# Masked attention with a feed-forward layer in float32 parts: the low part of k meets only the high part of q, as two 64-row matmuls, and eight feed-forward chunks are kept instead of eleven

## The chip, the cores and the metric

The kernel runs on one core of a Trainium2 chip. The metric is the device time of one execution in microseconds (us). The engines of the core are TensorE (PE, with its weight loads shown apart as PEld), VectorE (DVE), ScalarE (ACT), GpSimd (POOL) and SyncE (SP, which here only issues DMAs).

## The reference

Eight batches of eight heads, 576 positions, 64 numbers per head. A score survives only if it lies within tau = 0.02 of the greatest of its row; the rest of the row is masked. The result of attention, laid side by side by head, goes through a feed-forward layer with a leaky activation. All is float32 (the weights arrive as float64).

```python
scores = scale * np.matmul(q, k.transpose(0, 1, 3, 2))        # (8, 8, 576, 576), scale 1/8
thresh = np.max(scores, axis=-1, keepdims=True) - tau
scores = np.where(scores >= thresh, scores, -1000000000.0)
attn = np.exp(scores - np.max(scores, axis=-1, keepdims=True))
attn = attn / (np.sum(attn, axis=-1, keepdims=True) + 1e-09)
x = np.matmul(attn, v)                                        # heads side by side: (4608, 512)
h = x @ w_in                                                  # (512, 2048)
out = (np.maximum(h, 0.0) + alpha * np.minimum(h, 0.0)) @ w_out   # (4608, 512)
```

## The kernel before

**Parts.** A fast float32r matmul keeps only part of a float32's digits, so an operand is split into a high part (its rounded copy) and a low part (what is left), and products of parts are added in PSUM. For the scores of one head the stationary operand `qst` holds q's high part in rows 0 to 63 and q's low part in rows 64 to 127. The moving operands `kh` and `kl` hold the high and the low part of k, each twice, one above the other. So one 128-row matmul with `kh` gives (q high + q low) times k high, and one with `kl` gives (q high + q low) times k low.

**Pairs, units, cycles.** Two heads of one batch form a pair; there are 32 pairs. The 576 queries of each head are four chunks of 128 and a rest of 64; the two rests form one joint "tail" unit, so that a pair has nine units (`UNITS`). The attention loop runs over 288 cycles, one per unit, with a few before and behind. In cycle i it queues the masking of unit i, the scores of unit i+2, the row maximum and exponential of a unit ahead, the transposes of unit i (`turn`, `turn_k`, four or five 128-wide transposes by TensorE) and the copies of their results into parts (`hi`, `lo`). The scores of one unit are 576 keys as two halves of 288 columns in two PSUM banks: two matmuls with `kh`, two with `kl` (line 395); the tail has twice as many. `ps_s` holds the scores of two units.

**Beside the softmax.** In four of a pair's nine cycles the products with v are queued (`avmul`, line 542, the cycles `AVS`). The first four pairs (`WHOLE`) run them unsplit in float32 with a 128x64 stationary operand, all others in float32r parts with a 128x128 one. q, k and v of a later pair are loaded, split and moved into place at set cycles (`PREP`): `prep_qh`, `prep_qs` and `prep_ql` make q's parts (the low part in the tile `qt`), `move_q` and `move_q2` carry them by DMA from one half of the partitions to the other. The first pair is prepared by `prep_first`.

**The order of the work** on PE, ACT, DVE and POOL is written out by hand in the attention loop: each engine does its work in the order in which the loop queues it. SP's DMAs are in program order too.

**The planner of the feed-forward layer.** The 2048 hidden features are 16 chunks of 128. The first seven (`F1`) are worked off partly beside attention, for groups of 256 tokens, as soon as the batches they come from are done: layer 1 of one chunk is twelve 256-column matmuls (line 194, `pha`), layer 2 is 42 512-column matmuls per group, three parts by seven chunks by two halves (line 224, `acca`). `Mlp.cycle` decides in each cycle how much to queue. It holds a budget: `room` grows by `CYCLE` = 2.6 less the planned TensorE time of the cycle, `used`; a layer-1 chunk costs 1.31 of it, a layer-2 matmul 0.216. Its rule for layer 1, which also shows where the number of kept chunks enters:

```python
self.room = min(self.room, TH3) + CYCLE - used
if self.l1 and i >= self.gap and self.live < GB:
    ...
    elif slot and self.room > TH1 and ("i", fcs1[self.l1[0][2]]) in ready:
```

`live` counts chunks whose layer 1 is queued and whose second half of layer 2 is not; `GB` is both its limit and the number of buffers of the tile `g` (2 KB per partition each) that holds a chunk between the layers. `slot` is false in the four cycles with `avmul`.

**Behind attention.** `drain` does what the planner left of the first seven chunks, while the other nine chunks' weights are fetched and decoded from float64 (`Split64`, on ACT, DVE and POOL). Then the nine chunks are run for nine groups of 512 tokens (`phb`, `accb`). There the order is the compiler's scheduler's.

Of the kernel before, what the change touches and what calls it, by code (L numbers as in the profile page):

```python
# [11 lines left out]
F32R = mybir.dt.float32r  # L12
# [3 lines left out]
AF = mybir.ActivationFunctionType  # L16
ALU = mybir.AluOpType
AX = mybir.AxisListType
PSUM = bass.MemoryType.PSUM
DRAM = bass.MemoryType.DRAM  # L20

P = 128
D = 64
S = 576
NKC = 4
F1 = 7
G1 = 256
G2 = 512
# A float64's upper word read as a float32 orders values by magnitude. These two
# bounds are the words of the least normal float32 and of the largest one that  # L30
# still rounds to a finite 12-bit part.
WORD_LO = 2.0**-15
WORD_HI = 122876.0
ENGINES = {mybir.EngineType.PE, mybir.EngineType.Activation, mybir.EngineType.DVE, mybir.EngineType.Pool}
UNITS = [(0, 0), (0, 1), (1, 0), (1, 1), ("t", 0), (2, 0), (2, 1), (3, 0), (3, 1)]
GB = 11
ENG1 = ('vpp', 'vpp')
# [27 lines left out]
def f(ap):  # L65
    return ap.bitcast(F32)
# [3 lines left out]
def tile_masked_attention_moe(  # L70
# [11 lines left out]
    nc = tc.nc  # L82
# [19 lines left out]
    class Split64:  # L102
        """float64 bits -> hi + lo in float32r, to 24 bits or better."""

# [129 lines left out]
    at = ExitStack()  # L234
# [4 lines left out]
    KW = 2 * S + D  # L239
    qst_b = [ap1.tile([P, 2, S + D], F32R, name=f"qst{i}") for i in range(2)]  # L240
    for t in qst_b:
        nc.gpsimd.memset(f(t[:, :, S:]), 0.0)

    class Turned:
        """The transposed scores of two heads, in parts, with columns of ones that sum v."""

# [20 lines left out]
    class Pair:  # L267
        """The steps of two heads of one batch; each queues work on one or two engines."""

# [7 lines left out]
        def load(self, what):  # L277
            pi, b, hp = self.pi, self.b, self.hp
            if what == "v" and self.whole:
                self.vst = ap1.tile([P, 10, D], F32, tag="vst", name=f"vst{pi}", bufs=2)  # L280
                nc.sync.dma_start(self.vst, v[b, hp])
                return
            if what == "v":
                self.vr = ap1.tile([P, 10, D], F32, tag="raw", name=f"vr{pi}", bufs=2)
                nc.sync.dma_start(self.vr, v[b, hp])
                return
            src = (k if what == "k" else q)[b, hp]
            w = S + D if what == "k" else S
            if pi == 0:
                # The first pair's are doubled on the way in, so that its scores start at once.  # L290
                r = ap1.tile([P, KW if what == "k" else 2 * S], F32, tag="vst" if what == "k" else "p", name=f"{what}r{pi}", bufs=2)
                for j in range(2):
                    n = w if j else S
                    for half in range(2):
                        nc.sync.dma_start(r[half * D : (half + 1) * D, j * S : j * S + n], src[j * D : (j + 1) * D, :n])
                if what == "k":
                    self.kr = r
                else:
                    self.qr = r[:, : 2 * S].rearrange("p (a b) -> p a b", a=2)
                return  # L300
            if pi == 1:
                r = spool.tile([P, w], F32, name=f"{what}r{pi}")
            else:
                r = ap1.tile([P, w], F32, tag="raw", name=f"{what}r{pi}", bufs=2)
            nc.sync.dma_start(r, src[:, :w])
            if what == "k":
                self.kr = r
            else:
                self.qr = r

        def prep_first(self, j):
            """The splits of q and k for one head, before there is other work."""
            if j == 0:
                self.kh = ap1.tile([P, KW], F32R, tag="kh", name=f"kh{self.pi}", bufs=2)
                self.kl = ap1.tile([P, KW], F32R, tag="kl", name=f"kl{self.pi}", bufs=2)
                self.qst = qst_b[self.pi % 2]
            c = slice(0, S) if j == 0 else slice(S, KW)
            nc.scalar.activation(self.kh[:, c], self.kr[:, c], AF.Copy)
            nc.vector.tensor_tensor(self.kl[:, c], self.kr[:, c], f(self.kh[:, c]), op=ALU.subtract)
            qs = self.qst[:, j, :S]  # L320
            nc.scalar.activation(qs, self.qr[:, j], AF.Copy, scale=0.125)
            nc.vector.scalar_tensor_tensor(qs[D:], self.qr[D:, j], 0.125, f(qs[D:]), op0=ALU.mult, op1=ALU.subtract)

        # The two heads' q and k come one above the other. The parts are made so, and then moved:
        # qst holds the parts of q one above the other, kh and kl each part of k twice.
        def prep_kh(self):
# [16 lines left out]
        def prep_qh(self):  # L343
            self.qst = qst_b[self.pi % 2]
            nc.scalar.activation(self.qst[:, 0, :S], self.qr, AF.Copy, scale=0.125)

# [5 lines left out]
        def prep_ql(self):  # L352
            self.qt = ap1.tile([P, S], F32R, tag="qt", name=f"qt{self.pi}", bufs=1)
            if QLV and self.pi >= QLV:
                nc.vector.scalar_tensor_tensor(self.qt, self.qr, 0.125, f(self.qst[:, 0, :S]), op0=ALU.mult, op1=ALU.subtract)
                return
            nc.gpsimd.tensor_tensor(self.qt, self.qr, f(self.qst[:, 0, :S]), op=ALU.subtract)

        def move_q(self):
            nc.sync.dma_start(f(self.qst[:D, 1, :S]), f(self.qst[D:, 0, :S]))  # L360
            nc.sync.dma_start(f(self.qst[D:, 1, :S]), f(self.qt[D:]))

        def move_q2(self):
            nc.sync.dma_start(f(self.qst[D:, 0, :S]), f(self.qt[:D]))

# [10 lines left out]

        # A unit is (chunk of queries, head), or the tail: the last queries of the
        # first head above the first queries of the second.
        def scores(self, u):
            qc, j = UNITS[u]  # L380
            if u == 0:
                self.sm = ap1.tile([P, 9], F32, tag="sm", name=f"sm{self.pi}", bufs=2)
            qf = self.qst.rearrange("p a b -> p (a b)")
            key = lambda j, rot: (j * S + rot, j * S + rot + S)
            if qc == "t":
                stats = [(qf[:, NKC * P : S + D], key(0, 0)), (qf[:, S : S + P], key(1, D))]
            else:
                o = j * (S + 2 * D) + qc * P
                stats = [(qf[:, o : o + P], key(j, 0))]
            ps = ps_s.tile([P, 2, 512], F32, tag="s", name=f"s{self.pi}_{u}")  # L390
            n = len(stats)
            for ki, kk in enumerate((self.kh, self.kl)):
                for i, (w, (a, _)) in enumerate(stats):
                    for h in range(2):
                        nc.tensor.matmul(  # L395
                            ps[:, h, :288],
                            w,
                            kk[:, a + h * 288 : a + (h + 1) * 288],
                            start=(ki == 0 and i == 0),
                            stop=(ki == 1 and i == n - 1),  # L400
                        )
            self.S[u] = ps
# [39 lines left out]
        def turn_k(self, u):  # L442
            """The keys beyond the four blocks: of both heads at once for a chunk of queries."""
            qc, j = UNITS[u]
# [12 lines left out]
        def places(self, u):  # L457
            """(PSUM, its place in SBUF by part) for the unit's transposed blocks."""
            qc, j = UNITS[u]
# [96 lines left out]

        # Divide by the sums; rows that kept no score get the mean of v.
        def recip(self):
# [47 lines left out]

    # Where in a pair's nine cycles the work beside the softmax falls.
    for p in pairs:
        o = 9 * p.pi
        n = o - 9  # L610
# [36 lines left out]
    class Mlp:  # L647
        """The part of the MLP that runs beside attention, a little in each cycle."""

# [63 lines left out]
        def cycle(self, i, used, slot):  # L713
            """Work for the tensor engine up to the cycle's length."""
            self.room = min(self.room, TH3) + CYCLE - used
# [12 lines left out]
        def drain(self):  # L728
            """What is left when attention is done, in the scheduler's order."""
            for gi, st, fi in list(self.l1):  # L730
# [38 lines left out]
    nready = 0  # L769
    # The words of a piece of w_in wait where w_out's parts will be; those of w_out  # L770
    # in the place of its next chunk.
    pieces = []
# [18 lines left out]
    with tc.manual_schedule(engines=ENGINES) if ENGINES else ExitStack():  # L791
# [12 lines left out]
        for i in range(-3, total + TAIL):  # L804
# [17 lines left out]
            while nready < len(groups1) and sum(groups1[nready]) <= (i - RDY) // (9 * NPAIR) * S:  # L822
                mlp.ready(nready)
                nready += 1
            used = 0.92
            if unit(i + 2)[1] == 4:
                used += 0.49
            if unit(i)[1] in (1, 3, 4, 6, 8):
# [128 lines left out]
```

## Time and profile before

| | us |
|---|---|
| median of 3 runs | 1398.17 |
| lowest, highest | 1396.24, 1400.92 |
| span of the profiled execution | 1397.3 |
| DVE busy | 975.7 |
| ACT busy | 820.9 |
| POOL busy | 762.3 |

The profile is of one execution; its span, first instruction to last, is 0.9 us below the median of the runs, and no other time of that execution is given. Times of the trace are counted from the span's start. A matmul's duration in the trace is that from its start to a modelled end and holds the way through the array; matmuls overlap, so the time that one takes of TensorE is the distance between the starts (or the ends) of neighbours. A figure in brackets is the time an engine was idle before a row and what it waited for; "issue" means that the profile shows nothing it waited for.

### The profile page before, as it was taken

The numbers are of one execution on the slowest core, as the hardware profiler recorded it, in microseconds if no ns is written. First come the engines' busy times: TensorE is split into PE (matmuls) and PEld (weight loads), VectorE is DVE, ScalarE is ACT, GpSimd is POOL, SyncE is SP. The second block draws the span as 40 slices with busy tenths as digits, with TensorE's granted clock in tenths as the row PEclk, the third lists the DMA queues.
The fourth block names the chain that finished last, engine by engine and source line by source line (L and its number), as shares of the span: only waits on it lengthen the run. The fifth ranks groups of instructions, "written<-read, shape, count | busy, mean of one in ns | idle before, by whom it ended". The sixth has DMA issues, their size and how long they took to land.

```text
span 1397.3 us, 23301 instructions
## 1 busy us (share of the span) xinstructions
PE 1339.4 (96%) x8116; PEld 1181.2 (85%) x8116; DVE 975.7 (70%) x1933; ACT 820.9 (59%) x1843; POOL 762.3 (55%) x821
## 2 busy tenths in 40 slices
PE   5888899999999999999999999888999999999998
PEld 4556789999999999999999998777888888888887
DVE  6999988888888898898888957986323323323332
ACT  7788888888888888888888854453112012111100
POOL 3776676666676666576676557566434124223311
PEclk9999999999999999999999999999999999999999
DMA  8643634545545444454454214433320220111011
GB/s 249 184 127 106 180 105 122 162 116 142 147 117 150 139 134 131 132 154 127 128 160 132 83 57 153 132 109 128 121 74 17 91 91 33 59 61 42 19 61 38
DMA packets 94628, 157.67 MB, mean 113 GB/s; under 512 B 14160, under 2 KB 39024, under 8 KB 94512
## 3 DMA queue, kind: packets, MB, share of 16 engines
q1 hardware_dynamic: 94512, 156.19, 38.4%
q8 instruction: 65, 1.06, 0.3%
q14 instruction: 51, 0.42, 0.1%
HBM read 85.53 MB, written 28.46 MB: 82 GB/s over the span
## 4 chain that ended last, share of the span: by engine, by line
PE 80%; DVE 9%; ACT 4%; DMA 2%; issue 2%; POOL 2%; SPq 0%; DVEq 0%; POOLq 0%; ACTq 0%
PE phb L194 16%; PE accb L224 16%; PE s L395 10%; PE av L542 10%; PE acca L224 9%; PE pha L194 9%; PE t L439 7%; DVE p L430 2%; DVE nmx L410 2%; DMA wri<-in_moe_w_in_dram 1%; PE tk L455 1%; DVE wti L135 1%; POOL wi L152 1%; ACT xb L555 1%; ACT xa L553 1%
## 5 line engine op out<-in xcount | busy, mean ns | idle before, releaser
L410 DVE TENSOR_REDUCE nmx<-s 128x1 f32<-128x576 f32 x288 | 217.0, 753 | 72.6 <-PE s L395 69.5
L215 ACT ACTIVATE gb<-ptb 128x512 fp32r<-128x512 f32 x81 | 50.9, 630 | 337.7 <-DVE ptb L873 337.3
L218 POOL TENSOR_TENSOR gb<-ptb,gb 128x512 fp32r<-128x512 f32 x81 | 104.4, 1290 | 257.0 <-ACT gb L215 256.8
L224 PE MATMUL acca<-wo,ga 128*128 128x512 f32 x756 | 230.7, 419 | 7.2 <-ACT ga L215 4.0
L224 PE MATMUL accb<-wo,gb 128*128 128x512 f32 x972 | 221.9, 389 | 0.0
L224 PEld LDWEIGHTS accb<-wo,gb 128*128 128x128 f32 x972 | 182.4, 188 | 37.9
L430 DVE SCALAR_TENSOR_TENSOR p<-s,thr,p 128x576 f32<-128x576 f32 x256 | 206.6, 807 | 1.3 <-ACT thr L423 0.9
L194 PE MATMUL phb<-xh,wi 128*128 128x512 f32 x648 | 202.9, 392 | 1.1 <-ACT xh L180 1.1
L194 PE MATMUL pha<-xh,wi 128*128 128x256 f32 x1008 | 199.7, 284 | 3.7 <-DVE pta L873 3.4
L418 ACT ACTIVATE p<-s,nmx 128x576 f32<-128x576 f32 x256 | 190.0, 742 | 10.8 <-DVE nmx L410 10.5
L395 PE MATMUL s<-kh,qst 128*128 128x288 f32 x640 | 142.2, 312 | 38.1 <-DVE p L430 23.3
L194 PEld LDWEIGHTS pha<-xh,wi 128*128 128x128 f32 x1008 | 163.8, 190 | 9.9 <-DVE pta L873 4.6
L224 PEld LDWEIGHTS acca<-wo,ga 128*128 128x128 f32 x756 | 132.8, 191 | 28.6 <-ACT ga L215 5.3
L439 PE MATMUL t<-ident,p 128*128 128x128 f32 x1024 | 154.6, 274 | 0.0
L395 PEld LDWEIGHTS s<-kh,qst 128*128 128x128 f32 x640 | 101.4, 193 | 61.5 <-issue 29.4
L903 DVE TENSOR_TENSOR ob<-accb,pin 128x512 f32<-128x512 f32 x36 | 24.2, 689 | 181.9 <-PE accb L224 181.9
L194 PEld LDWEIGHTS phb<-xh,wi 128*128 128x128 f32 x648 | 122.6, 189 | 27.2 <-ACT xh L180 1.5
L194 PE MATMUL pha<-xl,wi 128*128 128x256 f32 x504 | 142.2, 282 | 0.0
L872 DVE TENSOR_SCALAR ptb<-phb,alpha_sb 128x512 f32<-128x512 f32 x81 | 60.7, 751 | 108.5 <-PE phb L194 96.4
L395 PE MATMUL s<-kl,qst 128*128 128x288 f32 x640 | 133.8, 299 | 0.0
L194 PE MATMUL phb<-xl,wi 128*128 128x512 f32 x324 | 127.2, 393 | 3.6 <-POOL xl L182 3.6
L439 PEld LDWEIGHTS t<-ident,p 128*128 128x128 f32 x1024 | 126.5, 141 | 0.1
(117 smaller groups left out, 2772.6 us busy)
## 6 DMA issues: line engine op xcount, KB each, us to landing
kr<-in_k_dram SPq DMA_DIRECT2D x31, 320.0 KB
rb<-rvd SPq DMA_DIRECT2D x64, 144.0 KB
xs<-xa SPq DMA_DIRECT2D x32, 288.0 KB
part<-po SPq DMA_DIRECT2D x36, 256.0 KB
pin<-part SPq DMA_DIRECT2D x36, 256.0 KB
out_dram<-ob SPq DMA_DIRECT2D x36, 256.0 KB
vr<-in_v_dram SPq DMA_DIRECT2D x28, 320.0 KB
qr<-in_q_dram SPq DMA_DIRECT2D x31, 288.0 KB
```

The lines of the kernel that those rows point to most:

```text
L194: nc.tensor.matmul(ph[:, :n], w[:, c, :], xx[:, c, :n], start=(c == 0 and ti == 0), stop=(c == NCC - 1 and ti == 2),)
L215: nc.scalar.activation(g[:, 0, :n], t[:, :n], AF.Copy)
L218: nc.gpsimd.tensor_tensor(g[:, 1, :n], t[:, :n], f(g[:, 0, :n]), op=ALU.subtract)
L224: nc.tensor.matmul(acc[:m, :], gg[:, g, o : o + m], w, start=(first and ti == 0), stop=(last and ti == 2))
L395: nc.tensor.matmul(ps[:, h, :288], w, kk[:, a + h * 288 : a + (h + 1) * 288], start=(ki == 0 and i == 0), stop=(ki == 1 and i == n - 1),)
L410: nc.vector.tensor_reduce(self.nmx[:, j : j + 1], self.S[u][0][:, :, :288], axis=AX.XY, op=ALU.max, negate=True)
L418: nc.scalar.activation(pj, ps[:, :, :288], AF.Exp, bias=nmx[:, j : j + 1], scale=1.0)
L430: nc.vector.scalar_tensor_tensor(pj, ps[:, :, :288], thr[:, j : j + 1], pj, op0=ALU.is_ge, op1=ALU.mult, accum_out=self.sm[:, c : c + 1])
L439: nc.tensor.transpose(tb[:, c, :], pt[:, j, j * D + c * P : j * D + (c + 1) * P], ident)
L542: nc.tensor.matmul(pa[:m, :n], w, x, start=(part == 0 and c == 0), stop=(part == z.parts[-1] and c == NKC))
L872: nc.vector.tensor_scalar(t[:, :n], ph[:, :n], 0.0, alpha_sb[:, fc : fc + 1], op0=ALU.min, op1=ALU.mult)
L903: nc.vector.tensor_tensor(ob[:m], acc[:m], pi_[:m], op=ALU.add)
```

## The change

The 128-row matmuls with `kl` are replaced. For the first 288 keys a 64-row matmul on rows 0 to 63 multiplies q's high part with `kl`; for the second 288 keys a 64-row matmul on rows 64 to 127 does the same with a second copy of q's high part, held in rows 64 to 127 of a new tile `q2`. Each writes its own PSUM bank. The product of q's low part with k's low part is no longer computed. The low part of q that was made in `qt` is now made in `q2` before the copy replaces it. `qst` changes its layout (one row of 2 x 576 + 64 instead of two of 576 + 64). Two DMAs per pair are added that fill `q2`, and in the first pair's preparation an activation. `GB` falls from 11 to 8. The planned TensorE time `used` falls from 0.92 to 0.79 per cycle, and its addition for the tail from 0.49 to 0.35. The diff without its changed comments:

```diff
-GB = 11
+GB = 8
...
-    qst_b = [ap1.tile([P, 2, S + D], F32R, name=f"qst{i}") for i in range(2)]
-    for t in qst_b:
-        nc.gpsimd.memset(f(t[:, :, S:]), 0.0)
+    qst_b = [ap1.tile([P, 2 * S + D], F32R, name=f"qst{i}") for i in range(2)]
+    q2_b = [ap1.tile([P, 2 * S + D], F32R, name=f"q2{i}") for i in range(2)]
+    for t in qst_b + q2_b:
+        nc.gpsimd.memset(f(t[:, S : S + D]), 0.0)
...
         def prep_first(self, j):
...
-            qs = self.qst[:, j, :S]
-            nc.scalar.activation(qs, self.qr[:, j], AF.Copy, scale=0.125)
-            nc.vector.scalar_tensor_tensor(qs[D:], self.qr[D:, j], 0.125, f(qs[D:]), op0=ALU.mult, op1=ALU.subtract)
+            qs = self.qst[:, j * (S + D) : j * (S + D) + S]
+            nc.scalar.activation(qs[:D], self.qr[:D, j], AF.Copy, scale=0.125)
+            q2 = self.q2[D:, j * (S + D) : j * (S + D) + S]
+            nc.scalar.activation(q2, self.qr[D:, j], AF.Copy, scale=0.125)
+            nc.vector.scalar_tensor_tensor(qs[D:], self.qr[D:, j], 0.125, f(q2), op0=ALU.mult, op1=ALU.subtract)
...
         def prep_ql(self):
-            self.qt = ap1.tile([P, S], F32R, tag="qt", name=f"qt{self.pi}", bufs=1)
+            self.qt = self.q2[:, :S]
...
         def move_q(self):
-            nc.sync.dma_start(f(self.qst[:D, 1, :S]), f(self.qst[D:, 0, :S]))
-            nc.sync.dma_start(f(self.qst[D:, 1, :S]), f(self.qt[D:]))
+            nc.sync.dma_start(f(self.qst[:D, S + D :]), f(self.qst[D:, :S]))
+            nc.sync.dma_start(f(self.qst[D:, S + D :]), f(self.qt[D:]))
+            nc.sync.dma_start(f(self.q2[D:, S + D :]), f(self.qst[D:, :S]))
 
         def move_q2(self):
-            nc.sync.dma_start(f(self.qst[D:, 0, :S]), f(self.qt[:D]))
+            nc.sync.dma_start(f(self.qst[D:, :S]), f(self.qt[:D]))
+            nc.sync.dma_start(f(self.q2[D:, :S]), f(self.qst[:D, :S]))
...
-            for ki, kk in enumerate((self.kh, self.kl)):
-                for i, (w, (a, _)) in enumerate(stats):
-                    for h in range(2):
-                        nc.tensor.matmul(
-                            ps[:, h, :288],
-                            w,
-                            kk[:, a + h * 288 : a + (h + 1) * 288],
-                            start=(ki == 0 and i == 0),
-                            stop=(ki == 1 and i == n - 1),
-                        )
+            for i, (o, (a, _)) in enumerate(stats):
+                for h in range(2):
+                    c = a + h * 288
+                    nc.tensor.matmul(ps[:, h, :288], self.qst[:, o : o + P], self.kh[:, c : c + 288], start=(i == 0), stop=False)
+            for i, (o, (a, _)) in enumerate(stats):
+                for h, w in enumerate((self.qst, self.q2)):
+                    c, r = a + h * 288, slice(h * D, (h + 1) * D)
+                    nc.tensor.matmul(ps[:, h, :288], w[r, o : o + P], self.kl[r, c : c + 288], start=False, stop=(i == n - 1))
...
-            used = 0.92
+            used = 0.79
             if unit(i + 2)[1] == 4:
-                used += 0.49
+                used += 0.35
```

More of the change, by code (lines that the diff above doesn't have):

```diff
@@ L316, in prep_first @@
                 self.qst = qst_b[self.pi % 2]
+                self.q2 = q2_b[self.pi % 2]
             c = slice(0, S) if j == 0 else slice(S, KW)
@@ L344, in prep_qh @@
             self.qst = qst_b[self.pi % 2]
-            nc.scalar.activation(self.qst[:, 0, :S], self.qr, AF.Copy, scale=0.125)
+            self.q2 = q2_b[self.pi % 2]
+            nc.scalar.activation(self.qst[:, :S], self.qr, AF.Copy, scale=0.125)
         def prep_qs(self):
@@ L352, in prep_ql @@
         def prep_ql(self):
-            self.qt = ap1.tile([P, S], F32R, tag="qt", name=f"qt{self.pi}", bufs=1)
+            self.qt = self.q2[:, :S]
             if QLV and self.pi >= QLV:
-                nc.vector.scalar_tensor_tensor(self.qt, self.qr, 0.125, f(self.qst[:, 0, :S]), op0=ALU.mult, op1=ALU.subtract)
+                nc.vector.scalar_tensor_tensor(self.qt, self.qr, 0.125, f(self.qst[:, :S]), op0=ALU.mult, op1=ALU.subtract)
                 return
-            nc.gpsimd.tensor_tensor(self.qt, self.qr, f(self.qst[:, 0, :S]), op=ALU.subtract)
+            nc.gpsimd.tensor_tensor(self.qt, self.qr, f(self.qst[:, :S]), op=ALU.subtract)
         def move_q(self):
-            nc.sync.dma_start(f(self.qst[:D, 1, :S]), f(self.qst[D:, 0, :S]))
-            nc.sync.dma_start(f(self.qst[D:, 1, :S]), f(self.qt[D:]))
+            nc.sync.dma_start(f(self.qst[:D, S + D :]), f(self.qst[D:, :S]))
+            nc.sync.dma_start(f(self.qst[D:, S + D :]), f(self.qt[D:]))
+            nc.sync.dma_start(f(self.q2[D:, S + D :]), f(self.qst[D:, :S]))
         def move_q2(self):
-            nc.sync.dma_start(f(self.qst[D:, 0, :S]), f(self.qt[:D]))
+            nc.sync.dma_start(f(self.qst[D:, :S]), f(self.qt[:D]))
+            nc.sync.dma_start(f(self.q2[D:, :S]), f(self.qst[:D, :S]))
         def prep_vh(self):
@@ L382, in scores @@
                 self.sm = ap1.tile([P, 9], F32, tag="sm", name=f"sm{self.pi}", bufs=2)
-            qf = self.qst.rearrange("p a b -> p (a b)")
             key = lambda j, rot: (j * S + rot, j * S + rot + S)
             if qc == "t":
-                stats = [(qf[:, NKC * P : S + D], key(0, 0)), (qf[:, S : S + P], key(1, D))]
+                stats = [(NKC * P, key(0, 0)), (S, key(1, D))]
             else:
-                o = j * (S + 2 * D) + qc * P
-                stats = [(qf[:, o : o + P], key(j, 0))]
+                stats = [(j * (S + 2 * D) + qc * P, key(j, 0))]
             ps = ps_s.tile([P, 2, 512], F32, tag="s", name=f"s{self.pi}_{u}")
             n = len(stats)
-            for ki, kk in enumerate((self.kh, self.kl)):
-                for i, (w, (a, _)) in enumerate(stats):
-                    for h in range(2):
-                        nc.tensor.matmul(
-                            ps[:, h, :288],
-                            w,
-                            kk[:, a + h * 288 : a + (h + 1) * 288],
-                            start=(ki == 0 and i == 0),
-                            stop=(ki == 1 and i == n - 1),
-                        )
+            for i, (o, (a, _)) in enumerate(stats):
[6 more added lines that the diff above has]
+                    nc.tensor.matmul(ps[:, h, :288], w[r, o : o + P], self.kl[r, c : c + 288], start=False, stop=(i == n - 1))
             self.S[u] = ps
```

## The prediction

> **What bounds the kernel now.** I read the head of the profile first, then a table of stretches of time, which shows that the span has four parts with different limits.
>
> ```profile
> span 1397.3 us, 23301 instructions
> core 0: us, PE busy (x) PEld busy (x) DVE busy (x) ACT busy (x) POOL busy (x), PEclk, DMA share, GB/s
> 0.00:200.00 200.00, 161.89 (x971) 125.92 (x972) 178.15 (x352) 162.30 (x370) 124.73 (x141) 0.99 0.57 163
> 200.00:800.00 600.00, 598.75 (x4372) 570.50 (x4371) 528.70 (x1174) 515.30 (x1230) 391.43 (x494) 1.00 0.48 134
> 800.00:830.00 30.00, 29.71 (x219) 28.10 (x218) 22.49 (x52) 20.27 (x51) 18.37 (x27) 1.00 0.16 47
> 830.00:960.00 130.00, 115.50 (x649) 98.01 (x648) 105.25 (x161) 56.96 (x104) 83.86 (x69) 0.96 0.40 127
> 960.00:1397.00 437.00, 433.53 (x1913) 358.66 (x1911) 141.08 (x199) 66.12 (x91) 143.91 (x91) 1.00 0.19 62
> ```
>
> From 200 to 830 us TensorE is never idle (598.75 of 600 us) while VectorE has 528.70: a microsecond of array time added or saved there is one of the span. Before 200 us TensorE idles 38 of 200 us and VectorE is the busiest, for it decodes weights beside attention. From 960 us on only the nine late chunks run, which the change does not touch. From 830 to 960 us TensorE idles again. The waits of TensorE in the first and the fourth part, and the shares of the chain of waits in the fourth, say for what:
>
> ```profile
> PE s L395 <- DVE p L430: 23.3, 23, 2.3
> PE acca L224 <- ACT ga L215: 4.0, 4, 2.3
> PE phb L194 <- POOL xl L182: 3.6, 1, 3.6
> by line: DMA wri<-in_moe_w_in_dram 12.9%; PE acca L224 8.6%; issue 7.3%; PE phb L194 7.1%; POOL wi L152 6.4%; DVE wti L127 4.8%; DMA xr<-xs 4.5%; DVE wti L135 3.8%; POOL xl L182 3.6%; DVE wri L148 3.4%; PE pha L194 3.3%; DVE wro L140 3.1%;
> ```
>
> Early on the scores wait for VectorE's mask, which frees their PSUM (23.3 us). In the fourth part the chain is led by fetching and decoding the late weights: some microseconds of TensorE work less there buy little.
>
> The next rows are groups of instructions by line: the first from 200 to 800 us, the other four from the start to 830.34 us.
>
> ```profile
> L410 DVE TENSOR_REDUCE nmx<-s 128x1 f32<-128x576 f32 x213 | 160.7, 754 | 61.3 <-PE s L395 58.3
> L395 PE MATMUL s<-kl,qst 128*128 128x288 f32 x640 | 133.8, 299 | 0.0
> L224 PE MATMUL acca<-wo,ga 128*128 128x512 f32 x518 | 169.3, 427 | 0.8 <-issue 0.8
> L194 PE MATMUL pha<-xh,wi 128*128 128x256 f32 x760 | 152.5, 284 | 0.2 <-ACT pra L207 0.2
> L194 PE MATMUL pha<-xl,wi 128*128 128x256 f32 x380 | 107.1, 282 | 0.0
> ```
>
> 213 row maxima in 600 us make a cycle 2.82 us. With the few cycles behind 800 us about 216 units, that is 24 pairs, lie in the TensorE-bound part, and 72 units before it. A cycle has 528.70 / 213 = 2.48 us of VectorE and 515.30 / 213 = 2.42 us of ScalarE.
>
> **Part 1: the matmuls saved.** The timeline of TensorE (start, us, operation) at a tail:
>
> ```profile
> 502.25 0.70 PE L395 MATMUL s<-kh,qst 128*128 128x288 f32 x4
> 502.79 0.68 PE L395 MATMUL s<-kl,qst 128*128 128x288 f32 x4
> 503.31 0.60 PE L439 MATMUL t<-ident,p 128*128 128x128 f32 x4
> ```
>
> Four `kl` matmuls take 503.31 - 502.79 = 0.52 us, 0.13 each. A pair has 640 / 32 = 20 of them. If two 64-row matmuls on the two halves run side by side, ten slots of 0.13 go: 1.3 us per pair.
>
> **Part 2: the switches between 128-row and 64-row use of the array, two per unit.** Nothing in this trace uses 64 rows. I bound the cost by the two places where the array is used in part by columns. The first is the float32 product with v of the first four pairs, on 64 columns. The rows show the last transpose ahead of such a group, its first matmul and that one's weight load, the whole group of six, its last matmul, and the score matmul behind it with its load; then, of the waits of weight loads, the two that belong here (total, times, longest).
>
> ```profile
> 59.17 0.27 PE L439 MATMUL t<-ident,p 128*128 128x128 f32 x1
> 59.38 0.48 PE L542 MATMUL av<-eo,vst 128*64 128x322 f32 x1
> 59.37 0.13 PEld L542 LDWEIGHTS av<-eo,vst 128*64 128x64 f32 x1 [0.17 <-ACT kh L328]
> 59.38 1.84 PE L542 MATMUL av<-eo,vst 128*64 128x322 f32 x6
> 60.78 0.43 PE L542 MATMUL av<-eo,vst 128*64 128x322 f32 x1
> 61.15 0.40 PE L395 MATMUL s<-kh,qst 128*128 128x288 f32 x1
> 61.15 0.19 PEld L395 LDWEIGHTS s<-kh,qst 128*128 128x128 f32 x1 [0.49 <-issue]
> 61.52 0.29 PE L395 MATMUL s<-kl,qst 128*128 128x288 f32 x1
> PEld av L542 <- issue: 5.0, 30, 0.2
> PEld s L395 <- issue: 29.4, 29, 2.7
> ```
>
> Elsewhere a weight load runs under the matmul before it. Here it starts only 0.07 us before the modelled end of the last matmul (59.17 + 0.27 = 59.44, load at 59.37; 60.78 + 0.43 = 61.21, load at 61.15), at the way in and at the way out, some 30 times each. The cost, end to end: the first matmul of the group ends at 59.86, 0.42 behind the transpose; the next five take (61.21 - 59.86) / 5 = 0.27 each; so 0.15 is lost. The score matmul ends at 61.55, 0.34 behind the group's last, where 0.13 is its slot: 0.20 is lost, and its duration is 0.40 instead of the usual 0.29 because its 128-column load lies bare; the group's first has 0.48 instead of 0.43 with a 64-column load. A way in with 128-column loads, as the change has, therefore costs 0.15 + 0.11 - 0.05 = 0.21, taken as 0.20.
>
> The second place is the tail's 64-column transpose:
>
> ```profile
> 812.36 0.60 PE L439 MATMUL t<-ident,p_t 128*128 128x128 f32 x4
> 812.79 0.27 PE L453 MATMUL tk_t<-ident,p_t 128*64 128x128 f32 x1
> 812.69 0.11 PEld L453 LDWEIGHTS tk_t<-ident,p_t 128*64 128x64 f32 x1
> 812.80 0.19 PEld L224 LDWEIGHTS acca<-wo,ga 128*128 128x128 f32 x1
> ```
>
> Its load runs under the transpose before it, the next load 0.01 us behind its own start: a switch for nothing. So the ends are 0 and 0.40 us per unit. I take 0.40. The `av` group is, like the changed scores, an ordinary product that adds up in PSUM on a part of the array; the transpose only passes data through. What speaks against it: the group is also plain float32, and nothing here separates that from its width. The Trainium skill, "TensorEngine Tiling (Array Packing)", Key Properties, states that changing the tiling mode, not just the tile, drains the TensorE; by that rule the sum is the one below; the `av` rows agree with it, the transpose rows do not.
>
> With 0.40: per pair 9 x 0.40 - 1.3 = +2.3 us, and over 24 pairs **+55 us**. In the first 72 units the bounds are 0 and 8 x 2.3 = 18 us. TensorE has 38 us of idle time there and VectorE sets the pace, so I take 2 us.
>
> **Part 3: eleven chunks to eight, and the planner's numbers.** The planner's counters depend on nothing that the chip does, so I followed `room`, `live` and the due times cycle by cycle. Before, they give 95 layer-1 chunks and 526 layer-2 matmuls up to the end of the loop; the rows above have (760 + 380) / 12 = 95 chunks and 518 matmuls up to the last product with v. After, with 8 and 0.79, they give 95 and 541. So the limit takes back in layer 1 what the smaller `used` would allow, and 15 layer-2 matmuls of about 0.23 us move from the fourth part, where TensorE has gaps, into the third: +3.4 us there, given back by half or so; I take +2. The order is lumpier: in every 36 cycles from 72 on about four stand at the limit of 8 and leave 5.0 us of the 2.6 us budgets unspent; before, none is unspent. With cycles of 3 us that costs nothing, since TensorE is still the longest; in the first rival it does not. In `drain` the next group can be only one chunk ahead instead of four; the decoding above covers that, 0 to 5 us if not; I take 0.
>
> **Part 4: the preparation.** The rows: ScalarE's share in the first pair and TensorE's wait there; the DMA issues of `move_q` and `move_q2`, and SP's own wait for the first of them.
>
> ```profile
> L321 ACT ACTIVATE qst<-qr 128x576 fp32r<-128x576 f32 x2 | 1.4, 682 | 1.8 <-DMA qr<-in_q_dram 1.8
> PE s L395 <- DVE qst L322: 11.1, 2, 10.8
> qst<-qt SPq DMA_DIRECT2D x62, 144.0 KB
> SPq L364 <- DMA qst<-qst: 25.9, 29, 2.0
> ```
>
> The two activations become four; one of 0.68 us per head. The first scores wait for this preparation, so up to 2 x 0.68; I take 0.7. For each later pair SP issues two more copies of 144 KB, 62 in all. `move_q2` already waits 25.9 / 29 = 0.9 us for `move_q`'s read; the added copies make it wait for two more reads, with the next loads of SP queued behind. The parts are due four cycles (11 us) later, and the DMA engines are busy 0.48 of the time: nothing. The same work on GpSimd goes into `q2` instead of `qt`; `q2` has two buffers, last read nine cycles ago: nothing.
>
> **Sum.** 55 + 2 + 2 + 0.7 = +60 us on the profiled 1397.3; the runs' median lies 0.9 above it, which I keep: 1398.2 + 60 = 1458 us. Its own range: 1440 (a way in as cheap as the `av` group's, 0.15, and all of the moved work given back: -11 and -3, and some stalls under other waits) to 1480 (the first pairs pay in full, +16, and the drain +5).
>
> **The rivals.**
>
> *No stall, side by side.* The switch is as free as at the transpose and the two matmuls take one slot. It decides as soon as a switch costs less than 0.07 us (half of 1.3 / 9). Then 24 x 1.3 = 31 us go. The cycle would be 2.82 - 0.14 = 2.67 us on TensorE, against 2.48 of VectorE and 2.42 of ScalarE, so the lumps cost: four cycles in 36 with little for TensorE run at VectorE's pace and lose up to 5.0 - 4 x 0.12 = 4.5 us, of which buffers of two units take most; I take 1.3, 8 us over the six periods. With the other terms: 1398 - 31 + 8 + 2 + 0.7 - 2 (early) = 1376 us; its range is 1362 to 1390. The Trainium skill, "TensorE: Matmul & The Clock Gate", Part 3, The mechanism, supports this one: it gives the time of row tiles packed together as one matmul's plus about 4 ns per further tile, by which the slots saved would be the full ones; no run here shows 64-row tiles.
>
> *No stall, but the two loads one after the other.* A 128-column load lasts 0.11 us bare (above), two 0.22 against 0.26 now: 0.04 to 0.05 saved by ten per pair, 24 pairs: -11 us, with +3 from parts 3 and 4: about 1390.
>
> *Bare loads without a full stop.* Loads at a switch cannot run ahead, but nothing waits for the array to empty: 0.11 twice per unit, 9 x 0.22 - 1.3 = 0.7 per pair: +17 us, 1416 with the rest.
>
> **How the numbers follow.** Full stall 0.50; no stall 0.32; loads in series 0.07; bare loads 0.11. The first has the most because it is the one ordinary product on a part of the array in this trace. The point is its 1458. A measurement of this kernel tells about 0.3% (4 us) from no change. Faster: all of the no-stall case and most of the serial loads, 0.38. Same: their edges, 0.04. Slower: 0.50 and nearly all of the 0.11, a bit less at the edges, 0.58. The range leaves out the lower third of the no-stall case (0.11) and the top of the stall case (0.06): 1372 to 1474; the likeliest case's own is 1440 to 1480.
>
> **What the changed profile would show.** The stall: idle time of "issue" ahead of the `kl` loads and ahead of the transposes' loads in every unit, first 64-row and first transpose matmul with about 0.11 us more duration, and row maxima from 200 to 800 us down from 213 to about 195. No stall: the two 64-row matmuls of a unit start within 0.02 us, transposes follow 0.13 behind, and about 222 row maxima. Loads in series: their starts 0.11 apart. Planner: 541 `acca` matmuls and 95 chunks before the loop ends. Wrong altogether I would be if the fourth part grew by more than 5 us, or if VectorE's waits for GpSimd's or SP's new work showed up between 200 and 800 us.

## The result and the profile after

The changed kernel takes 1480.8 us (median of 4 runs, 1477.4 to 1481.6) against 1399.4 us before (median of 4 runs): 1.0576 times as long, 95% interval 1.0558 to 1.0593. The forecast was slower, 1458 us with a range of 1372 to 1474: the sign is right, but the loss is 81 us instead of 60 and the time lies above the range. Two causes of nearly equal size stand behind it, and the prediction had only one of them.

Below are the stretches of time of both kernels, cut at the same places of the work: the first row maximum of the ninth pair, the last product with v, the first layer-2 matmul of the late chunks. The first fence is the changed kernel, the second the one before.

```profile
span 1478.9 us, 23496 instructions
core 0: us, PE busy (x) PEld busy (x) DVE busy (x) ACT busy (x) POOL busy (x), PEclk, DMA share, GB/s
0.00:222.00 222.00, 192.31 (x1068) 132.03 (x1068) 190.22 (x376) 174.09 (x400) 132.06 (x154) 0.98 0.57 161
222.00:906.00 684.00, 666.87 (x4505) 573.18 (x4503) 542.34 (x1197) 526.68 (x1252) 399.31 (x508) 0.99 0.46 129
906.00:1051.00 145.00, 119.57 (x679) 103.84 (x677) 110.97 (x171) 61.60 (x110) 92.14 (x76) 0.94 0.40 128
1051.00:1479.00 428.00, 424.25 (x1872) 350.98 (x1870) 135.07 (x190) 61.30 (x84) 136.77 (x87) 1.00 0.18 58
```
```profile
0.00:213.00 213.00, 174.89 (x1069) 138.44 (x1070) 189.35 (x377) 172.86 (x398) 133.38 (x155) 0.99 0.55 156
213.00:830.00 617.00, 615.46 (x4491) 586.08 (x4490) 539.99 (x1197) 525.01 (x1252) 401.14 (x508) 1.00 0.47 131
830.00:969.00 139.00, 124.50 (x688) 105.49 (x687) 111.87 (x171) 59.58 (x108) 90.74 (x74) 0.96 0.42 132
969.00:1397.00 428.00, 424.53 (x1873) 351.18 (x1872) 134.46 (x190) 63.50 (x86) 137.03 (x86) 1.00 0.18 59
```

The first eight pairs take 9 us more, the TensorE-bound pairs 67, the part behind attention 6, the late chunks nothing: 82 us. In the second part TensorE's busy time grew by 51 us, and 17 us of idle time came up where there had been 1.5. Where most of the growth in busy time comes from is seen in a unit of the changed kernel (timeline of TensorE, then of its weight loads):

```profile
503.14 0.29 PE L401 MATMUL s<-kh,qst 128*128 128x288 f32 x1
503.37 0.40 PE L406 MATMUL s<-kl,qst 64*128 64x288 f32 x1
503.37 0.39 PE L406 MATMUL s<-kl,q 64*128 64x288 f32 x1
503.70 0.33 PE L444 MATMUL t<-ident,p 128*128 128x128 f32 x1
503.37 0.18 PEld L406 LDWEIGHTS s<-kl,qst 64*128 64x128 f32 x1 [0.17 <-issue]
503.37 0.18 PEld L406 LDWEIGHTS s<-kl,q 64*128 64x128 f32 x1
503.70 0.42 PEld L444 LDWEIGHTS t<-ident,p 128*128 128x128 f32 x4
```

The two 64-row matmuls and their two loads start together. But both loads start 0.06 us before the modelled end of the `kh` matmul (503.14 + 0.29 = 503.43), and the transposes' load 0.07 before the end of the 64-row ones (503.77): the signature of the float32 group before. A load that starts so late lies bare: it no longer runs under a matmul. From the end of the last `kh` matmul to that of the 64-row ones it is 503.77 - 503.43 = 0.34 us here and 0.33 on average over this part; less the slot of 0.13, the way in costs 0.20. The way out takes 504.03 - 503.77 = 0.26, less a transpose's 0.11: 0.15.

The idle time shows in the waits of TensorE. The first line is the changed kernel from 220 to 868 us, the next two are all that the kernel before has from 213 to 830 us, the last has the row maxima of the changed kernel from 200 to 800 us (213 before):

```profile
PE s L401 <- DVE p L435: 15.8, 11, 1.4
PE acca L224 <- issue: 0.8, 2, 0.5
PE pha L194 <- ACT pra L207: 0.2, 1, 0.2
L415 DVE TENSOR_REDUCE nmx<-s 128x1 f32<-128x576 f32 x193 | 146.1, 757 | 104.1 <-PE s L406 99.8
```

Eleven times the scores wait 1.4 us for the mask, and a twelfth time before 906 us. Before there was no such wait. The first group of experiments separates the two causes.

### The profile page after: what moved, and what is told of

It reads as the page before. It is cut to its first block, busy times and chain, and to the rows that moved or that the text cites. A ratio compares the mean times of both kernels' runs of the same rounds, so it can differ in the third digit from the quotient of the medians.

```text
span 1478.9 us, 23496 instructions
## 1 busy us (share of the span) xinstructions
PE 1403.0 (95%) x8116; PEld 1160.0 (78%) x8116; DVE 978.6 (66%) x1933; ACT 823.7 (56%) x1845; POOL 760.3 (51%) x823
## 4 chain that ended last, share of the span: by engine, by line
PE 82%; DVE 10%; DMA 2%; issue 2%; ACT 2%; POOL 1%; SPq 0%; POOLq 0%; DVEq 0%; ACTq 0%
PE accb L224 15%; PE phb L194 14%; PE av L547 12%; PE t L444 10%; PE pha L194 9%; PE acca L224 9%; PE s L406 6%; PE s L401 6%; DVE p L435 2%; DVE nmx L415 2%; DMA wro<-in_moe_w_out_dram 1%; PE tk L460 1%; DVE wti L135 1%; DVE wto L127 1%; DVE wto L135 1%
## 5 line engine op out<-in xcount | busy, mean ns | idle before, releaser
L224 PE MATMUL acca<-wo,ga 128*128 128x512 f32 x756 | 222.0, 414 | 1.1 <-POOL ga L218 1.1
L401 PE MATMUL s<-kh,qst 128*128 128x288 f32 x640 | 145.3, 318 | 46.8 <-DVE p L435 33.9
L444 PE MATMUL t<-ident,p 128*128 128x128 f32 x1024 | 171.1, 291 | 0.0
L444 PEld LDWEIGHTS t<-ident,p 128*128 128x128 f32 x1024 | 109.2, 142 | 37.6 <-issue 6.0
L211 POOL TENSOR_TENSOR pta<-pta,pra 128x256 f32<-128x256 f32 x95 | 70.0, 737 | 101.7 <-ACT pra L207 101.7
```

Source lines behind the costliest of these rows:

```text
L211: nc.gpsimd.tensor_tensor(t[:, :n], t[:, :n], r[:, :n], op=ALU.add)
L224: nc.tensor.matmul(acc[:m, :], gg[:, g, o : o + m], w, start=(first and ti == 0), stop=(last and ti == 2))
L401: nc.tensor.matmul(ps[:, h, :288], self.qst[:, o : o + P], self.kh[:, c : c + 288], start=(i == 0), stop=False)
L444: nc.tensor.transpose(tb[:, c, :], pt[:, j, j * D + c * P : j * D + (c + 1) * P], ident)
```

## The experiments

**Group 1: the change taken apart.** Theory A says that the switches cost most of the 81 us; rival B says that the eight chunks and the copies do.

Only the planner's numbers (*plan_only*), on the kernel before:

```diff
-GB = 11
+GB = 8
-            used = 0.92
+            used = 0.79
...
-                used += 0.49
+                used += 0.35
```

> The kernel before with only the planner's three numbers of the change (8 chunks, 0.79, 0.35); the scores stay 128-row matmuls. Theory A (each of the two switches per unit empties the array, about 0.34 us per unit against 0.13 saved; besides, the planner's new numbers make some cycles without feed-forward work, in which TensorE waits for the mask): the same 1.5 us waits of the scores for the mask in every second pair as in the changed kernel, some 16 us, and about 6 us more behind attention: 1415 to 1425 us. Rival B (the switches are cheap, the loss of 81 us is that of the eight chunks and of the copies): 1440 us or more.

1440.8 us, 1.029 (1.026 to 1.032), where A had 1415 to 1425. Half of the loss needs neither 64 rows nor copies; so far B is right. The eleven waits are there (214 to 827 us),

```profile
PE s L395 <- DVE p L430: 20.4, 11, 1.9
```

and a pair takes 26.61 us instead of 25.33. The waits are 20.4 of the 29 us that these 23 pairs lose; the rest was not taken apart.

Only the 64-row matmuls (*rows_only*), on the kernel before:

```diff
-            for ki, kk in enumerate((self.kh, self.kl)):
...
+            for i, (w, (a, _)) in enumerate(stats):
+                for h in range(2):
+                    c = a + h * 288
+                    nc.tensor.matmul(ps[:, h, :288], w, self.kh[:, c : c + 288], start=(i == 0), stop=False)
+            for i, (w, (a, _)) in enumerate(stats):
+                for h in range(2):
+                    c, r = a + h * 288, slice(h * D, (h + 1) * D)
+                    nc.tensor.matmul(ps[:, h, :288], w[r], self.kl[r, c : c + 288], start=False, stop=(i == n - 1))
```

> The kernel before with the low part of k in two 64-row matmuls per unit and nothing else: 11 chunks, 0.92, no second tile and no copies; the second half of the keys is multiplied with q's low part instead of its high part, so its scores' low terms are not those wanted. Theory A: 24 pairs x (9 x 0.34 - 1.3) = +42 us and some 6 us in the first pairs: 1440 to 1452 us. Rival B: 1365 to 1400 us.

1443.6 us, 1.031 (1.029 to 1.032), as theory A said: a pair takes 26.82 us, and between 222 and 839 us TensorE is hardly ever idle:

```profile
222.00:839.00 617.00, 616.69 (x4241) 529.57 (x4240) 516.40 (x1137) 503.57 (x1195) 380.73 (x479) 1.00 0.46 128
```

The two add up: 41 + 44 = 85 us, where the change costs 81. Per pair 1.28 + 1.49 = 2.77, and the changed kernel has 28.09 - 25.33 = 2.76.

The changed kernel without the switches (*copies*):

```diff
-                for h, w in enumerate((self.qst, self.q2)):
-                    c, r = a + h * 288, slice(h * D, (h + 1) * D)
-                    nc.tensor.matmul(ps[:, h, :288], w[r, o : o + P], self.kl[r, c : c + 288], start=False, stop=(i == n - 1))
+                for h in range(2):
+                    c = a + h * 288
+                    nc.tensor.matmul(ps[:, h, :288], self.qst[:, o : o + P], self.kl[:, c : c + 288], start=False, stop=(i == n - 1))
```

> The changed kernel with the low part of k again in two 128-row matmuls on the stacked parts of q: the planner's numbers, the second tile and its copies stay, the switches go. Theory A: as the planner's numbers alone, within 4 us. Rival B: 1440 us or more. A third reading, that the added copies on SP's queue cost: 5 to 15 us above the planner's numbers alone.

1441.4 us, 0.7 more than the planner's numbers alone: the second tile and its 62 copies cost nothing that can be measured.

The changed kernel with one 128-row matmul in place of the two 64-row ones, as a stand-in for a free switch (*one_slot*); the second half of the keys gets no low part:

```diff
-                    nc.tensor.matmul(ps[:, h, :288], self.qst[:, o : o + P], self.kh[:, c : c + 288], start=(i == 0), stop=False)
+                    nc.tensor.matmul(ps[:, h, :288], self.qst[:, o : o + P], self.kh[:, c : c + 288], start=(i == 0), stop=(h == 1 and i == n - 1))
...
-                for h, w in enumerate((self.qst, self.q2)):
-                    c, r = a + h * 288, slice(h * D, (h + 1) * D)
-                    nc.tensor.matmul(ps[:, h, :288], w[r, o : o + P], self.kl[r, c : c + 288], start=False, stop=(i == n - 1))
+                c = a
+                nc.tensor.matmul(ps[:, 0, :288], self.qst[:, o : o + P], self.kl[:, c : c + 288], start=False, stop=(i == n - 1))
```

> The changed kernel with a single 128-row matmul for the low part of k, on the first 288 keys; the second 288 keys get no low part. This is what two 64-row matmuls side by side would cost if a switch were free. Theory A: 31 us under the changed kernel without switches (copies), about 1376 to 1395 us. If the freed slot is not the bound (VectorE and the waits for the mask are): no less than copies.

1414.4 us, 27 under *copies* where 31 were expected; the 1376 to 1395 named were missed, because *copies* itself was dearer than thought. It is still 1.010 (1.008 to 1.012) times the kernel before: with its planner numbers the change would have lost even if the switch were free.

**Group 2: which of the planner's numbers, and is it the switch.** Theory C puts the planner's loss down to the lowered planned time, theory D to the limit of eight chunks.

Only 0.79 and 0.35, eleven chunks (*used79*):

```diff
-            used = 0.92
+            used = 0.79
...
-                used += 0.49
+                used += 0.35
```

> The kernel before with the planned TensorE time lowered as in the change (0.79, 0.35) and 11 chunks kept. Followed through the planner's counters: 96 chunks and 538 layer-2 matmuls up to the loop's end, and one cycle in 18 (where a group's x is loaded) left with 1.8 us of its 2.6 us budget unspent, because layer 2 ran ahead and has nothing left. Theory C (the lowered planned time makes the planner run ahead and then dry, which costs the wait for the mask): as with all the planner's numbers, 1432 to 1445 us, with eleven waits of about 2 us between 213 and 826 us. Theory D (the limit of 8 chunks does it): within 5 us of the kernel before.

1438.7 us, 1.029 (1.025 to 1.032), with fifteen waits between 213 and 830 us:

```profile
PE s L395 <- DVE p L430: 20.9, 15, 2.1
```

Only the limit (*gb8*):

```diff
-GB = 11
+GB = 8
```

> The kernel before with 8 chunks kept and the planned time as before (0.92, 0.49). By the counters 78 chunks and 428 layer-2 matmuls instead of 95 and 526 up to the loop's end: 17 x 1.42 + 98 x 0.23 = 47 us of TensorE work move behind attention. Theory C: attention gets shorter by part of that and the part behind it longer, 1398 to 1420 us. Theory D: 1435 us or more.

1445.9 us, 1.033 (1.031 to 1.035): dearer than C allowed, and what D named. The 47 us of work moved behind attention made that part 188 us long instead of 139 (first row, 828 to 1016 us), but attention ended only 2 us earlier: 34 waits for the mask, 27.8 us in all, took most of the room (second and third row, 213 to 830 us):

```profile
828.00:1016.00 188.00, 170.91 (x995) 148.06 (x994) 132.98 (x207) 70.94 (x133) 113.14 (x96) 0.98 0.36 114
PE s L395 <- DVE p L430: 24.4, 29, 1.6
PE s L395 <- DVE p_t L430: 3.4, 5, 0.7
```

So the planned time alone costs 39 us, the limit alone 46, and both together 41. Each theory fails on the other's run: C and D were both too simple.

Four switches per unit instead of two (*two_trips*), on *rows_only*:

```diff
-            for i, (w, (a, _)) in enumerate(stats):
-                for h in range(2):
+            for h in range(2):
+                for i, (w, (a, _)) in enumerate(stats):
                     c = a + h * 288
                     nc.tensor.matmul(ps[:, h, :288], w, self.kh[:, c : c + 288], start=(i == 0), stop=False)
-            for i, (w, (a, _)) in enumerate(stats):
-                for h in range(2):
+                for i, (w, (a, _)) in enumerate(stats):
```

> As rows_only (64-row matmuls alone, 11 chunks, 0.92; the second half of the keys is multiplied with q's low part), but in the order kh, kl, kh, kl, so that each unit switches four times instead of twice and the two 64-row matmuls lie apart. Theory A (the switch costs): per unit 0.13 + 0.33 + 0.33 + 0.33 + 0.26 against 0.13 + 0.13 + 0.33 + 0.26 us, 0.53 more, times 216 units and some of the first 72: 1555 to 1590 us. If the 64-row matmul itself is dear and the switch is not: 0.13 more per unit, about 1470 us.

1596.2 us. A pair takes 31.58 us, 4.75 more than in *rows_only*: 0.53 per unit, the sum of the prices to the digit. The first eight pairs paid 37 us more, which put the time above the expected range. Every step is a switch:

```profile
499.93 0.29 PE L395 MATMUL s<-kh,qst 128*128 128x288 f32 x1
500.16 0.40 PE L398 MATMUL s<-kl,qst 64*128 64x288 f32 x1
500.48 0.40 PE L395 MATMUL s<-kh,qst 128*128 128x288 f32 x1
500.81 0.40 PE L398 MATMUL s<-kl,qst 64*128 64x288 f32 x1
501.14 0.66 PE L436 MATMUL t<-ident,p_t 128*128 128x128 f32 x4
```

All of the scores in 64-row matmuls (*all64*), on *rows_only*:

```diff
-            for i, (w, (a, _)) in enumerate(stats):
-                for h in range(2):
-                    c = a + h * 288
-                    nc.tensor.matmul(ps[:, h, :288], w, self.kh[:, c : c + 288], start=(i == 0), stop=False)
-            for i, (w, (a, _)) in enumerate(stats):
-                for h in range(2):
-                    c, r = a + h * 288, slice(h * D, (h + 1) * D)
-                    nc.tensor.matmul(ps[:, h, :288], w[r], self.kl[r, c : c + 288], start=False, stop=(i == n - 1))
+            for ki, kk in enumerate((self.kh, self.kh, self.kl)):
+                for i, (w, (a, _)) in enumerate(stats):
+                    for h in range(2):
+                        c, r = a + h * 288, slice(h * D, (h + 1) * D)
+                        nc.tensor.matmul(ps[:, h, :288], w[r], kk[r, c : c + 288], start=(ki == 0 and i == 0), stop=(ki == 2 and i == n - 1))
```

> As rows_only, but all of the scores in 64-row matmuls: three side-by-side pairs per unit (k high twice, k low once), one way in and one way out as before; the upper half of q's parts alone is used for the first keys and the lower half alone for the second, so the scores are not those wanted. Theory A with loads that run ahead inside the 64-row mode: 0.33 + 0.13 + 0.13 + 0.26 per unit, 0.85 as in rows_only: 1438 to 1450 us. Theory A with loads that cannot run ahead when the same rows are busy (the tail of the changed kernel has 0.235 us between two such pairs): 0.33 + 0.235 + 0.235 + 0.26 = 1.06, 0.2 more per unit: 1485 to 1510 us.

1437.5 us (26.85 per pair): the first theory, to half a microsecond below its range. Three side-by-side pairs of matmuls cost one way in and one way out. Four of the 64-row matmuls' loads fit into 0.30 us, so the second two lie under the first matmuls, of the same rows (TensorE, then the loads):

```profile
501.20 0.54 PE L396 MATMUL s<-kh,qst 64*128 64x288 f32 x4
501.57 0.29 PE L396 MATMUL s<-kl,qst 64*128 64x288 f32 x2
501.20 0.30 PEld L396 LDWEIGHTS s<-kh,qst 64*128 64x128 f32 x4
```

The price is that of the switch and not of 64 rows.

**Group 3: what makes the waits.** In *plan_only* one of them looks like this (TensorE, then VectorE):

```profile
404.43 0.43 PE L395 MATMUL s<-kh,qst 128*128 128x288 f32 x2
404.69 0.43 PE L395 MATMUL s<-kl,qst 128*128 128x288 f32 x2
404.96 0.60 PE L439 MATMUL t<-ident,p 128*128 128x128 f32 x4
407.41 0.50 PE L395 MATMUL s<-kh,qst 128*128 128x288 f32 x2 [1.85 <-DVE p L430]
406.45 0.81 DVE L430 SCALAR_TENSOR_TENSOR p<-s,thr,p 128x576 f32<-128x576 f32 x1
```

From 404.43 on TensorE has one cycle's scores and transposes, no products with v and nothing of the feed-forward layer: 1.1 us, in a cycle that takes VectorE 2.4. The next scores need the PSUM buffer that the next mask frees, and that ends at 407.3. They come every 18 cycles.

The first attempt to remove them (*copies_smooth*) took as its measure the budget that the planner's counters leave unspent, on *copies*; *smooth* is the same on the changed kernel:

```diff
-TH1, TH2, TH3 = 0.75, -0.45, 0.1
+TH1, TH2, TH3 = 0.3, -0.9, 0.1
-L2O = 3
+L2O = 2
-            used = 0.79
+            used = 0.88
...
-                used += 0.35
+                used += 0.45
```

> As copies (the changed kernel with the low part of k in 128-row matmuls), with four planner numbers set so that, by the counters, the same 95 chunks and 541 layer-2 matmuls are spread without a dry spell: used 0.88 and 0.45, TH1 0.3, TH2 -0.9, L2O 2; the cycle that loads a group's x and the one behind it keep 0.7 us of their budget unspent instead of 2.4. Theory C (dry cycles cost the 41 us): most of the eleven waits of about 2 us go; 1405 to 1418 us. If something else of the planner's numbers costs (8 chunks by themselves, the part behind attention): 1430 us or more.

> The changed kernel with the same four planner numbers as copies_smooth. Theory A and C together: 1441 minus 1399 us of planner loss shrinks, the switches' 37 to 44 us stay: 1445 to 1462 us. If the two do not add up: 1470 us or more.

1428.2 and 1473.3 us: misses, with 17.1 and 11.6 us of the same waits left from 213 to 800 us. (The 45 us between the two are the switches again, so those still add up.) The measure was wrong. By the counters, the cycle that loads a group's x still had neither layer-1 nor layer-2 work nor products with v; the budget seemed spent only because the cycles before had overdrawn it, and TensorE's earlier work cannot fill a later cycle in which it waits for a mask. Counted so, by cycles from 72 on whose TensorE work is over 0.6 us below VectorE's 2.45, there are none in the kernel before, 12 with the change's numbers, 12 in *copies_smooth*, 17 in *used79*, 19 in *gb8*. The traces bear this out: in the TensorE-bound part of the changed kernel, of *plan_only* and of *copies_smooth* there are twelve cycles, 18 apart, without feed-forward matmuls and products with v, and behind each of them, and nowhere else, the scores wait for the mask. Only in *gb8* is it not the whole: about half of its waits, none over 0.6 us, follow cycles that have one layer-1 chunk or the products with v alone. A setting with eight chunks and no such cycle (*copies_nodry* on *copies*, *nodry* on the changed kernel):

```diff
-TH1, TH2, TH3 = 0.75, -0.45, 0.1
+TH1, TH2, TH3 = 0.75, 0.2, 0.1
-L2O = 3
+L2O = 2
-            used = 0.79
+            used = 0.88
...
-                used += 0.35
+                used += 0.45
```

> As copies (128-row matmuls, 8 chunks), with planner numbers 0.88, 0.45, TH2 0.2 and L2O 2. By the counters 94 chunks and 539 layer-2 matmuls, and no cycle from 72 on whose TensorE work is over 0.6 us below VectorE's 2.45; with the change's numbers, and still with copies_smooth, there are 12, always the cycle that loads a group's x with no layer-2 work left. Theory E (such a cycle costs a wait for the mask of about 2 us): no such waits between 213 and 800 us, 25.3 to 25.5 us per pair, 1402 to 1412 us. If the eight chunks themselves cost: 1420 us or more.

> The changed kernel with the planner numbers of copies_nodry. Theories A and E: the switches' price alone is left, as in rows_only, and some 5 us behind attention: 1443 to 1455 us. If the waits come back with the longer cycle: 1465 us or more.

1408.4 us, 1.006 (1.004 to 1.007), and 1452.9 us, 1.038 (1.036 to 1.039). The empty cycles and the waits are gone, and *copies_nodry* needs 25.38 us per pair, with eight chunks:

```profile
215.00:798.00 583.00, 582.90 (x4247) 555.34 (x4246) 516.21 (x1138) 502.94 (x1194) 382.43 (x481) 1.00 0.53 148
```

So 33 of the planner's 41 us were the empty cycles. The other 8 stay, most of them behind attention: from the last product with v to the end it is 573 us, against 566.6 before. And 44.5 us lie between these two kernels: the switches, as in *rows_only*.

**The gain that was there** (*slot_only*), on the kernel before:

```diff
-            for ki, kk in enumerate((self.kh, self.kl)):
...
+            for i, (w, (a, _)) in enumerate(stats):
+                for h in range(2):
+                    c = a + h * 288
+                    nc.tensor.matmul(ps[:, h, :288], w, self.kh[:, c : c + 288], start=(i == 0), stop=(h == 1 and i == n - 1))
+            for i, (w, (a, _)) in enumerate(stats):
+                nc.tensor.matmul(ps[:, 0, :288], w, self.kl[:, a : a + 288], start=False, stop=(i == n - 1))
```

> The kernel before with a single 128-row matmul per unit for the low part of k, on the first 288 keys (the second get none), with 11 chunks and 0.92: a free switch with the planner left alone. Theory A and C: 24 x 1.3 = 31 us less, 1364 to 1374 us. If VectorE or the waits for the mask take over once TensorE has a slot less: 1385 us or more.

1378.5 us, 0.984 (0.982 to 0.986): between the two. The slots go, but TensorE's loads now wait longer for ScalarE's results (209 to 773 us),

```profile
PEld pha L194 <- ACT pra L207: 7.8, 22, 0.5
PEld tk L451 <- ACT xb L551: 5.7, 18, 0.4
```

and 22.6 of the 31 us arrive. That these waits, 0.9 and 1.9 us in the kernel before, are the whole of the difference was not tested. None of the versions with 64-row matmuls comes under the kernel before, and the one that does leaves out half of the low part.

## Why the prediction was right and wrong

*The likeliest case was the one that came.* The float32 product with v on 64 columns was the right row to go by, the free 64-column transpose the wrong one. The Trainium skill's rule in "TensorEngine Tiling (Array Packing)", Key Properties, that a change of tiling mode drains the TensorE, agrees with the 64-row rows here. The tail's 64-column transposes stay free in the changed kernel too, 0.11 us each.

The other two rivals fell as well: the two loads start together, not 0.11 apart, and a way in or out costs 0.20 or 0.15, not the 0.11 of a bare load alone. (The 1416 us of the bare-load rival leaves out some 4 us of its "rest".)

*The price.* Predicted 0.20 + 0.20 per unit, measured 0.20 + 0.15: the way out ends at transposes, and only 0.06 us of their load lies bare (first transpose 0.33 long instead of 0.27), where I had taken the score matmul's 0.11. By these prices a pair would lose 9 x 0.35 - 1.3, about 1.8 us; in *rows_only* it loses 1.49. Part of the difference was given back by loads of TensorE that had waited for ScalarE in the kernel before (213 to 796 us),

```profile
PEld tk L455 <- ACT xb L555: 1.9, 6, 0.3
PEld pha L194 <- ACT pra L207: 0.9, 4, 0.2
```

and no longer do in *rows_only*; the rest is open. In the TensorE-bound part that makes 36 us (24 x 1.49) instead of 55. The first pairs gave 9 us of their bound of 18 where I took 2. Together 44 instead of 57. The preparation, taken at 0.7, cost nothing: the longest wait for it is 10.8 us as before.

*The step that failed is part 3, the planner.* I took +2 us for it; alone it measures 41. That the time missed the range by no more than 7 us is luck: the price of the switches, 13 us too high, hid a third of this error. The counts were right: the changed trace has 94 chunks and 539 layer-2 matmuls up to the last product with v, where the counters gave 95 and 541 to the loop's end. I even wrote that cycles were left with unspent budget. The error is the sentence "with cycles of 3 us that costs nothing, since TensorE is still the longest". TensorE is the longest on average; in a cycle without other work it has 1.1 us, and it cannot go on, because the scores have two PSUM buffers and the next one comes free with the mask. I had also put those cycles down to the limit of eight; *used79* has 17 of them with eleven chunks.

*The rivals.* The no-stall case fell with the first rows of the new trace. Its 1376 us was wrong besides: its stand-in *one_slot* took 1414, by the same mis-sized step, and with the planner left alone (*slot_only*) 1378. The Trainium skill, "TensorE: Matmul & The Clock Gate", Part 3, The mechanism, gives packed row tiles one matmul's time plus some nanoseconds. The two here do start together (503.37 both), so the trace agrees inside the mode; what that model leaves out is the way in and out.

*Behind attention* the part grew by 6 us, just past the 5 that I had named as a sign of error. It comes with the planner's numbers, too: in *plan_only* that part is 144 us long as in the changed kernel, in *rows_only* 139 as before. The largest of its new waits is one of TensorE for `ptb`; what shifted there in the scheduler's order was not tried.

```profile
PE phb L194 <- DVE ptb L878: 9.7, 1, 9.7
```

Not settled: why the first eight pairs pay 9 us in *rows_only* and only 2 in *all64*, which has as many switches.

## What to carry to other kernels

The 64-row matmuls here were free only while the work stayed in them: count the ways in and out (0.35 us here for both) against the slots saved between them (0.13 each), and take the price from a group in the trace whose weight loads start only at the end of the matmul before. A planner's estimate is part of the kernel: when it is changed together with the work, run it by itself. And ask of a bound engine what it has to do in each cycle, not on average: with two buffers, TensorE here could not make up in the next cycle what it did not get in one.

## What the runs showed of the hardware that was not expected

Inside the 64-row use, the loads of the next two matmuls run under the matmuls of the same rows (four loads from 501.20 to 501.50, the matmuls to 501.74), and a further pair takes the 0.13 us of one 128-row matmul (*all64*). The stall was the same for two ways of cutting the array and two data types: 0.20 us into 64 rows in float32r, and 0.20 out of 64 columns in float32, each where a 128-column load lies bare.
